# A one-token decoder step: most of W2 moves into the ring of the key and value loads, and heads 28 and 29 are loaded in smaller pieces

## The chip, the cores and the metric

The kernel runs on 1 core of a Trainium2 chip. The metric is device time in microseconds (us) of one execution; of several runs the median is taken. The profile comes from one further execution, and its times count from the first instruction of that execution (its span).

## What is computed

Two layers with the same weights, each an attention block over a cache and then an MLP, for one token of width 640 (32 heads of 128, 8192 cached positions, hidden width 1728). All is fp32.

```python
def _A_ref(x, k_cache, v_cache, wq, wo):          # x: 1 x 1 x 640
    q = (x @ wq).reshape(B, Sq, H, Dh).transpose(0, 2, 1, 3)
    scores = jnp.einsum("bhqd,bhkd->bhqk", q, k_cache) * (Dh ** -0.5)
    p = _softmax(scores, axis=-1)
    o = jnp.einsum("bhqk,bhkd->bhqd", p, v_cache)
    return o.transpose(0, 2, 1, 3).reshape(B, Sq, H * Dh) @ wo
def _B_ref(x, w1, w2):                            # hidden width 1728
    return jnp.einsum("bsf,fd->bsd", jnp.maximum(jnp.einsum("bsd,df->bsf", x, w1), 0), w2)
x = x + _A_ref(_layernorm(x), A_k_cache, A_v_cache, A_wq, A_wo)
x = x + _B_ref(_layernorm(x), B_w1, B_w2)
x = x + _A_ref(_layernorm(x), A_k_cache, A_v_cache, A_wq, A_wo)
x = x + _B_ref(_layernorm(x), B_w1, B_w2)
```

Each layer reads the whole cache once: 32 heads with 4096 KB of keys and 4096 KB of values each.

## The kernel before, in words

**Heads and units.** Layer 1 (L = 0 in the code) takes the heads 0 to 31, layer 2 (L = 1) takes them from 31 down to 0. For a head, TensorE first multiplies the query with the keys (`scores`, L336), VectorE and ScalarE make the exponentials (L347, L349), TensorE turns them (L357), and then multiplies them with the values (`values`, L390). The table `UNITS` says in which loads a head comes: `WHOLE` is one load of keys and one of values, 4096 KB each; `HALVES` is four of 2048 KB; `LAST` splits the values into 2048, 1024, 512 and 512 KB. Before the change heads 0, 1, 29, 30 and 31 come in finer loads, the others whole.

**The ring.** One SBUF tile, `ring`, takes all keys and values. It is counted in units of 4 KB (8 floats in each of 128 partitions); a head's keys are 1024 units, and the ring has 3800. `todo` lists the loads in the order of their use; `place` looks for a free stretch for the next one, and `pump` issues loads on SyncE's queue (SP) as long as one fits. A load is issued in program order, so one that doesn't fit yet holds back all behind it. `release` is called after the matmuls of a piece (one of a head's four key runs or four value blocks); it frees the piece's place and calls `pump`. In layer 1 the streamed loads use the places 0 to 3071, three loads of 1024 units.

**What is kept.** The last 3800 units of layer 1 (all of head 31, and of head 30 all but two small key loads, `DROPPED`) stay in the ring, and layer 2 begins with them without a new load. So from the end of layer 1's loads the ring is full, and the first load of layer 2 that needs a place (head 29) can be issued only when layer 2 has used the first two key pieces of head 31. The two small key loads of head 30 go beside the ring, into tiles that the MLP has finished with (`load_beside` into `mix` and `wct`, L140).

**The weights.** `wq` and `wo` are loaded by groups of four heads, W1 and W2 once, all on ScalarE's queue (ACT). W1 and W2 stay in SBUF for both layers: `w1_t`, and `w2_t` with 14 row blocks of 128 x 640 floats, 4480 KB, loaded while layer 1 is at its eighth head (L557).

**The end of a layer.** After the last head's values come its output, the last column of the projection and the hidden layer (`hidden`, L470), then 14 blocks of the product with W2 (`times_rows`, L304, into `po`) in the order 0 to 3, 12, 13, 4 to 11; between them stand two steps of the layer norm (L261, L274). One block is 4 matmuls of 160 columns (two instructions each in the trace). Then the next layer's norm and its first queries (L284) follow.

Of the kernel before, what the change touches and what calls it, by code (L numbers as in the profile page):

```python
# [10 lines left out]
F32 = mybir.dt.float32  # L11
# [4 lines left out]
P = 128  # L16
D = 640
H = 32
# [17 lines left out]
K_ALL = [(r, 0, RUN) for r in range(4)]  # L36
V_ALL = [(b, 0, 4) for b in range(NBL)]
WHOLE = [("k", K_ALL), ("v", V_ALL)]
HALVES = [("k", K_ALL[:2]), ("k", K_ALL[2:]), ("v", V_ALL[:2]), ("v", V_ALL[2:])]
LAST = [("v", V_ALL[:2]), ("v", V_ALL[2:3]), ("v", [(3, 0, 2)]), ("v", [(3, 2, 2)])]  # L40
UNITS = {h: WHOLE for h in range(H)}
UNITS[0] = HALVES[:2] + LAST
UNITS[1] = HALVES
UNITS[29] = HALVES
UNITS[30] = [
    ("k", [(0, 432, 80), (1, 0, 80)]),
    ("k", [(0, 0, 432)]),
# [1 line left out]
] + HALVES[2:]  # L49
UNITS[31] = HALVES[:2] + LAST  # L50
DROPPED = {30: 2}
RING = 3800
MIX_AT = [12, 16, 20, 24]


def wide(kind, piece):

    return 4 * piece[2] * (1 if kind == "k" else DH) // 8


def size(unit):
    return sum(wide(unit[0], piece) for piece in unit[1])
# [4 lines left out]
F_TILES = 3  # L67
F_REST = 2
FB = 4 * F_TILES + F_REST


@with_exitstack
def decode_kernel(ctx: ExitStack, tc: tile.TileContext, x, kv, wq, wo, w1, w2, out):
# [16 lines left out]
    assert sum(size(UNITS[h][i]) for h, i in kept) == RING  # L90
    todo = [(0, u) for u in order]
    todo += [(1, (h, i)) for h in range(H)[::-1] for i in range(len(UNITS[h])) if (h, i) not in kept]

    beside = todo[len(order) : len(order) + 2]
    del todo[len(order) : len(order) + 2]
    dram_at, o = {}, 0
    for h, i in order:
        dram_at[h, i] = o
        o += 8 * P * size(UNITS[h][i])
    live = {}  # L100
    at_of = {}

    def place(layer, n):


        step = 512 if n % 512 == 0 else 8
        low, high = (0, RING) if layer else ((3072, RING) if n == RING - 3072 else (0, 3072))
        at, best = low, None
        for a, m in sorted(live.values()) + [(high, 0)]:
            a = min(a, high)  # L110
            if a - at >= n and (best is None or a - at < best[1]):
                best = at, a - at
            at = max(at, -(-(a + m) // step) * step)
        return None if best is None else best[0]

    def pump():
        while todo:
            layer, u = todo[0]
            kind, pieces = unit = UNITS[u[0]][u[1]]
            n = size(unit)  # L120
            at = place(layer, n)
            if at is None:
                return
            todo.pop(0)
            o = dram_at[u]
            nc.sync.dma_start(
                ring[:, 8 * at : 8 * (at + n)],
                kv[o : o + 8 * P * n].rearrange("(p m) -> p m", p=P),
            )
            for t, piece in enumerate(pieces):  # L130
                m = wide(kind, piece)
                live[layer, u, t] = at, m
                at_of[layer, u, t] = ring, 8 * at
                at += m

    def load_beside(where, at, n):
        layer, u = beside.pop()
        kind, pieces = UNITS[u[0]][u[1]]
        assert 8 * size(UNITS[u[0]][u[1]]) == n
        nc.sync.dma_start(  # L140
            where[:, at : at + n],
            kv[dram_at[u] : dram_at[u] + P * n].rearrange("(p m) -> p m", p=P),
        )
# [49 lines left out]
    blocks = ident.rearrange("p (g r) -> p g r", g=4)[:, :, :4]  # L193
# [6 lines left out]
    all_rows = one_of_each.to_broadcast([P, P])  # L200

    w1_t = consts.tile([P, NB, DFF], F32, name="w1_t")
    w2_t = consts.tile([P, FB, D], F32, name="w2_t")
    mix = consts.tile([P, DFF], F32, name="mix")
    wct = consts.tile([P, NB, P], F32, name="wct")

# [94 lines left out]
    def times_rows(acc, wt, col, first, last):  # L301

        for g in range(4):
            nc.tensor.matmul(  # L304
                acc[32 * g : 32 * g + 32, :DR],
                col.to_broadcast([col.shape[0], 32]),
                wt[:, g * DR : (g + 1) * DR],
                start=first,
                stop=last,
                skip_group_check=True,  # L310
            )
# [167 lines left out]
    def attention_and_mlp(L, xr, s):  # L479
# [60 lines left out]
        def due(h):  # L540

            where = heads.index(h)
            k, j = divmod(where, HG)
            if j == 0:
                o_cols[k] = work.tile([P, HG], F32, name="o_cols", bufs=2)
            if where and j == 0:
                chores.append([run_out(k - 1), "pe"])
            if j == 2 and k + 1 < NG:
                slow.append([queries_of(k + 1), "pe"])
            if where == H - 2:  # L550
                chores.append([first_of_last(), "pe"])
# [18 lines left out]
        for where, h in enumerate(heads):  # L570
# [27 lines left out]
            if h == last:  # L598
                o = work.tile([P, 1], F32, name="c_ol")
# [4 lines left out]
            else:  # L604
                k, j = divmod(where, HG)
# [45 lines left out]
        nb = 4 * F_TILES  # L651
# [11 lines left out]
        po = ps_m.tile([P, 512], F32, name="px")  # L663
        blocks = list(range(4)) + [nb, nb + 1] + list(range(4, nb))
        for a, b in enumerate(blocks):
            if a == 2:
                ss = deviations(x1, s1)
            if a == 8:
                r1 = spread_of_rows(ss)
            rows = 2 * half if b == nb + 1 else P  # L670
            times_rows(
                po, w2_t[:rows, b], hT[:rows, b : b + 1], a == 0, a == len(blocks) - 1
            )

        x2 = work.tile([P, DR], F32, name="xr", bufs=2)
        s2 = work.tile([P, 1], F32, name="x_s", bufs=2)
# [7 lines left out]
    for L in range(2):  # L684
# [22 lines left out]
def _laid_out(A_x, A_k_cache, A_v_cache, A_wq, A_wo, B_w1, B_w2):  # L707
    k = np.asarray(A_k_cache)[0].reshape(H, 4, 4, RUN, DH).transpose(0, 4, 1, 2, 3)
    v = np.asarray(A_v_cache)[0].reshape(H, 4, 4, NBL, P, DH).transpose(0, 4, 1, 2, 3, 5)
    kv = np.empty(H * P * SK * 2, k.dtype)  # L710
    o = 0
    for h in range(H):
        for kind, pieces in UNITS[h]:
            n = 8 * sum(wide(kind, piece) for piece in pieces)
            block = kv[o : o + P * n].reshape(P, n)
            o += P * n
            a = 0
            for piece in pieces:
# [9 lines left out]
    w2 = np.zeros((P, FB, D), np.asarray(B_w2).dtype)  # L728
    for b, f in enumerate(_hidden_rows()):
        w2[f >= 0, b] = np.asarray(B_w2)[f[f >= 0]][:, _COLS]  # L730
    return {
        "x": np.repeat(np.asarray(A_x).reshape(D)[_COLS].reshape(4, DR), 32, axis=0),
        "kv": kv,
        "wq": np.asarray(A_wq).reshape(NB, P, NG, HG * DH).transpose(2, 1, 0, 3),
        "wo": np.asarray(A_wo)[:, _COLS].reshape(NG, HG, DH, D).transpose(0, 2, 1, 3),
        "w1": np.asarray(B_w1).reshape(NB, P, DFF).transpose(1, 0, 2),
        "w2": w2,
    }


# [22 lines left out]
```

## Time and profile before

| | |
|---|---|
| time, three runs | 1376.2, 1380.74 and 1384.16 us, median 1380.74 |
| the profiled execution | span 1375.5 us; no other time of it is given |
| TensorE (PE) busy | 996.9 us (72%), mean granted clock 0.786 |
| VectorE, ScalarE busy | 174.7 us (13%), 100.4 us (7%) |
| DMA | 571.41 MB, mean 415 GB/s over the span |
| layer 1 ends, layer 2 begins | last W2 matmul of layer 1 at 715.6 us, first keys of layer 2 at 721.1 us |

Columns of the views: a group of instructions has its line, engine, operation, output <- inputs, shape and count, then busy time and mean, then the idle time before it with what ended it. A window has its length, the busy time of each engine (with the number of instructions), the granted TensorE clock, the busy share of the 16 DMA engines and their GB/s. A DMA issue has its queue, count, size and the time from issue to landing. SPq and ACTq are the queues of SyncE and ScalarE.

### The profile page before, as it was taken

How to read it: one execution, taken by the hardware profiler on the slowest of the kernel's cores; microseconds unless marked ns; L12 is line 12 of the kernel's file. 1: busy time of each engine (PE TensorE's matmuls, PEld its weight loads, DVE VectorE, ACT ScalarE, POOL GpSimd, SP SyncE). 2: the span in 40 equal slices, each digit the busy share in tenths (PEclk: the TensorE clock that was granted, in tenths of full speed). 3: DMA queues.
4: the chain of work that ended last, by engine and by line, in shares of the span. 5: the costliest groups of instructions: out<-in, count | busy, mean ns of one | idle time of the engine just before them, and what ended most of it. 6: DMA issues, size and time to landing. Idle time of an engine off the chain costs nothing.

```text
span 1375.5 us, 15829 instructions
## 1 busy us (share of the span) xinstructions
PE 996.9 (72%) x7136; PEld 386.9 (28%) x7136; DVE 174.7 (13%) x678; ACT 100.4 (7%) x273; POOL 2.9 (0%) x10
## 2 busy tenths in 40 slices
PE   5674746677677776877788757687777677788777
PEld 2221312222222222322243222232222322232223
DVE  1010100111111111111121111011110111111111
ACT  0000000000000000000001000000000000000000
POOL 0000000000000000000000000000000000000000
PEclk9676768887887878878798887677878877687879
DMA  9999999999999999999948999999999999999994
GB/s 395 435 429 430 428 431 430 432 429 432 428 431 432 427 433 433 427 433 422 428 190 361 431 429 428 431 430 428 433 433 426 431 430 431 431 430 432 430 423 196
DMA packets 26572, 571.41 MB, mean 415 GB/s; under 512 B 2948, under 2 KB 3080, under 8 KB 4616
## 3 DMA queue, kind: packets, MB, share of 16 engines
q1 hardware_dynamic: 21896, 524.02, 88.9%
q10 hardware_dynamic: 4608, 46.37, 8.1%
q8 instruction: 56, 0.92, 0.3%
q14 instruction: 12, 0.10, 0.0%
HBM read 570.38 MB, written 0.00 MB: 415 GB/s over the span
## 4 chain that ended last, share of the span: by engine, by line
DMA 68%; PE 29%; DVE 2%; ACT 1%; issue 1%; SPq 0%; ACTq 0%; DVEq 0%
DMA ring<-in_kv 68%; PE ps L336 10%; PE outs L390 10%; PE px L457 2%; PE pt L357 2%; PE px L284 1%; PE acc L304 1%; ACT p L349 1%; DVE h_t L347 1%; PE px L304 1%; PE acc L470 1%; PE pm L377 1%; PE pm L408 0%; DVE pT L365 0%; PE px L296 0%
## 5 line engine op out<-in xcount | busy, mean ns | idle before, releaser
L336 PE MATMUL ps<-ring,spread_q 128*32 128x512 f32 (+1 forms) x2056 | 340.8, 792 | 202.9 <-DMA ring<-in_kv 202.4
L390 PE MATMUL outs<-ring,pT 128*4 128x512 f32 (+1 forms) x2080 | 329.7, 787 | 37.9 <-DMA ring<-in_kv 37.7
L336 PEld LDWEIGHTS ps<-ring,spread_q 128*32 128x32 f32 x2056 | 68.1, 136 | 351.7 <-DMA ring<-in_kv 211.3
L390 PEld LDWEIGHTS outs<-ring,pT 128*4 128x4 f32 x2080 | 57.8, 102 | 248.4 <-issue 200.0
L347 DVE TENSOR_REDUCE h_t<-ps 128x1 f32<-128x512 f32 x64 | 44.3, 692 | 498.6 <-PE ps L336 498.6
L349 ACT ACTIVATE p<-ps,h_t 128x512 f32<-128x512 f32 x64 | 44.0, 687 | 711.0 <-DVE h_t L347 700.3
L408 PE MATMUL pm<-h_t,p 128*128 128x1 f32 x512 | 68.2, 254 | 34.2 <-DVE p L403 34.2
L408 PEld LDWEIGHTS pm<-h_t,p 128*128 128x128 f32 x512 | 62.7, 190 | 96.8 <-DVE p L403 96.8
L357 PE MATMUL pt<-row_of,p 128*128 128x16 f32 x512 | 70.9, 271 | 23.0 <-ACT p L349 22.9
L357 PEld LDWEIGHTS pt<-row_of,p 128*128 128x128 f32 x512 | 64.8, 198 | 35.1 <-ACT p L349 35.1
L403 DVE COPY p<-outs 128x256 f32<-128x256 f32 x64 | 27.2, 424 | 341.9 <-PE outs L390 341.9
L370 PE MATMUL pm<-ident,h_t 128*128 128x128 f32 x128 | 31.8, 331 | 44.2 <-DVE h_t L347 44.2
L404 ACT COPY p<-outs 128x256 f32<-128x256 f32 x64 | 23.8, 372 | 480.9 <-DVE p L403 480.9
L370 PEld LDWEIGHTS pm<-ident,h_t 128*128 128x128 f32 x128 | 19.4, 190 | 103.0 <-DVE h_t L347 100.4
L457 PE MATMUL px<-w_t,wct 128*128 128x448 f32 (+1 forms) x80 | 45.8, 659 | 0.0
L377 PE MATMUL pm<-h_t 128*128 128x1 f32 x128 | 27.8, 286 | 24.5 <-DVE h_t L374 24.5
L284 PE MATMUL px<-wq_t,ln_xc 128*32 128x128 f32 x640 | 34.6, 393 | 1.4 <-DMA wq_t<-in_wq 1.4
L284 PEld LDWEIGHTS px<-wq_t,ln_xc 128*32 128x32 f32 x640 | 29.2, 165 | 20.2 <-issue 17.1
L304 PE MATMUL acc<-wo_t,o_cols 128*32 128x160 f32 x496 | 32.8, 430 | 0.0
L377 PEld LDWEIGHTS pm<-h_t 128*128 128x128 f32 x128 | 22.3, 218 | 30.8 <-DVE h_t L374 30.8
L304 PEld LDWEIGHTS acc<-wo_t,o_cols 128*32 128x32 f32 x496 | 23.0, 163 | 23.7 <-issue 18.3
L365 DVE COPY pT<-pt 128x64 f32<-128x64 f32 x64 | 14.4, 225 | 75.0 <-PE pt L357 75.0
(97 smaller groups left out, 228.7 us busy)
## 6 DMA issues: line engine op xcount, KB each, us to landing
ring<-in_kv SPq DMA_DIRECT2D x108, 4096.0 KB, 25.3
ring<-in_kv SPq DMA_DIRECT2D x27, 2048.0 KB, 27.3
wq_t<-in_wq ACTq DMA_DIRECT2D x14, 1280.0 KB, 17.1
wo_t<-in_wo ACTq DMA_DIRECT2D x14, 1280.0 KB, 17.8
w_t<-in_w ACTq DMA_DIRECT2D x1, 4480.0 KB, 24.5
w_t<-in_w ACTq DMA_DIRECT2D x1, 4320.0 KB, 24.7
ring<-in_kv SPq DMA_DIRECT2D x3, 1024.0 KB, 25.6
ring<-in_kv SPq DMA_DIRECT2D x6, 512.0 KB, 28.5
```

The source lines that it names most:

```text
L284: nc.tensor.matmul(pq[32 * j : 32 * j + 32, :DH], xc[:, c : c + 1].to_broadcast([P, 32]), wq_t[g][:, c, j * DH : (j + 1) * DH], start=(c = ...
L304: nc.tensor.matmul(acc[32 * g : 32 * g + 32, :DR], col.to_broadcast([col.shape[0], 32]), wt[:, g * DR : (g + 1) * DR], start=first, stop=last,
L336: nc.tensor.matmul(hd.ps[32 * g : 32 * g + 32, c : c + n], spread_q[:, 3 - r : 35 - r], tile_of[:, at + g * n : at + (g + 1) * n], start=f ...
L347: nc.vector.tensor_reduce(hd.nm, hd.ps, AX.X, ALU.max, negate=True)
L349: nc.scalar.activation(hd.p, hd.ps, AF.Exp, bias=hd.nm, scale=1.0, accum_out=hd.l)
L357: nc.tensor.matmul(pt[:, 16 * b : 16 * b + 16], hd.p[:, b * P : (b + 1) * P], row_of.rearrange("p g r -> p (g r)"), start=True, stop=True,)
L370: nc.tensor.matmul(pt[:, :P], hd.nm.to_broadcast([P, P]), ident, start=True, stop=True)
L377: nc.tensor.matmul(pt[:, :1], hd.l.to_broadcast([P, P]), hd.wi, start=True, stop=True)
L390: nc.tensor.matmul(hd.out[32 * g : 32 * g + 4, r : r + m].rearrange("p r d -> p (r d)"), hd.pT[:, 4 * i : 4 * i + 4], tile_of[:, v : v + m ...
L403: nc.vector.tensor_copy(oc[:, :2], hd.out[:, :2])
L408: nc.tensor.matmul(pt[:, :1], oc[:, r], hd.w[:, r : r + 1], start=(r == 0), stop=(r == 3))
L457: nc.tensor.matmul(pt[:, :n], wct[:, c], w1_t[:, c, f : f + n], start=(c == 0), stop=(c == NB - 1),)
```

## The change

Twelve of W2's fourteen blocks (3840 KB) leave the resident tile; `w2_t` keeps the last two. The ring grows by the same 960 units to 4760. The twelve blocks become four loads (4, 4, 2 and 2 blocks) that stand in `todo` behind the last values of each layer, so W2 is read from HBM twice. In layer 1 they go to the places 3800 to 4759, which nothing else uses in that layer; in layer 2 every load may take any place. When a W2 block has been multiplied, its place is released like that of a key piece, and layer 2's first loads can take it. Head 28 is now loaded in halves, and head 29 in seven loads: keys 2048, 1792 and 256 KB, values four times 1024 KB, so that its first two key loads together (960 units) are as large as W2's places.

```diff
-UNITS[29] = HALVES
+UNITS[28] = HALVES
+UNITS[29] = [
+    ("k", K_ALL[:2]),
+    ("k", [(2, 0, 512), (3, 0, 384)]),
+    ("v", V_ALL[:1]),
+    ("v", V_ALL[1:2]),
+    ("k", [(3, 384, 128)]),
+    ("v", V_ALL[2:3]),
+    ("v", V_ALL[3:]),
+]
...
-RING = 3800
+KEPT = 3800
+W2_RUNS = [range(0, 4), range(4, 8), range(8, 10), range(10, 12)]
+UNITS["w2"] = [("w", list(run)) for run in W2_RUNS]
+W2_ALL = [("w2", i) for i in range(len(W2_RUNS))]
+RING = KEPT + 4 * F_TILES * D // 8
...
+    beside = [(1, u) for u in order if u[0] == 30 and u not in kept]
+    todo = [(0, u) for u in order + W2_ALL]
+    todo += [
+        (1, (h, i))
+        for h in range(H)[::-1]
+        for i in range(len(UNITS[h]))
+        if (h, i) not in kept and h != 30
+    ]
+    todo += [(1, u) for u in W2_ALL]
...
-        low, high = (0, RING) if layer else ((3072, RING) if n == RING - 3072 else (0, 3072))
+        if layer:
+            low, high = 0, RING
+        elif u[0] == "w2":
+            low, high = KEPT, RING
+        else:
+            low, high = (3072, KEPT) if n == KEPT - 3072 else (0, 3072)
...
-    w2_t = consts.tile([P, FB, D], F32, name="w2_t")
+    w2_t = consts.tile([P, F_REST, D], F32, name="w2_t")
...
-                nc.scalar.dma_start(w2_t, w2)
+                nc.scalar.dma_start(w2_t, w2_rest)
...
-            times_rows(
-                po, w2_t[:rows, b], hT[:rows, b : b + 1], a == 0, a == len(blocks) - 1
-            )
+            if b < nb:
+                i = next(i for i, run in enumerate(W2_RUNS) if b in run)
+                where = L, ("w2", i), b - W2_RUNS[i][0]
+                tile_of, at = at_of[where]
+                wt = tile_of[:, at : at + D]
+            else:
+                wt = w2_t[:rows, b - nb]
+            times_rows(po, wt, hT[:rows, b : b + 1], a == 0, a == len(blocks) - 1)
+            if b < nb:
+                release(*where)
```

The rows below are the program's instructions on one engine, in order; a width of 8192 means 8192 floats in each of 128 partitions, or 4096 KB. On SP's queue, from the second keys of head 30 in layer 1 over the change of layers into the loads of head 29 in layer 2, there stood before:

```order
L126 DMA ring<-in_kv 128x5824
L126 DMA ring<-in_kv 128x4096 x5
L126 DMA ring<-in_kv 128x2048
L126 DMA ring<-in_kv 128x1024 x2
L140 DMA mix<-in_kv 128x1728
L140 DMA wct<-in_kv 128x640
L126 DMA ring<-in_kv 128x4096 x4
L126 DMA ring<-in_kv 128x8192 x54
```

The same place now, from the last values of head 31 to the last small load of head 29 (`in_w` is W2's twelve blocks):

```order
L153 DMA ring<-in_kv 128x2048
L153 DMA ring<-in_kv 128x1024 x2
L153 DMA ring<-in_w 128x2560 x2
L153 DMA ring<-in_w 128x1280 x2
L164 DMA mix<-in_kv 128x1728
L164 DMA wct<-in_kv 128x640
L153 DMA ring<-in_kv 128x4096
L153 DMA ring<-in_kv 128x3584
L153 DMA ring<-in_kv 128x2048 x2
L153 DMA ring<-in_kv 128x512
L153 DMA ring<-in_kv 128x2048 x2
L153 DMA ring<-in_kv 128x4096 x4
```

W2 stands between the last values and the loads into `mix` and `wct`; the four halves of head 29 have become seven loads, and the four halves behind them are head 28. At the end of the program, the same queue held before, from the last whole loads to the output:

```order
L126 DMA ring<-in_kv 128x8192 x54
L126 DMA ring<-in_kv 128x4096 x7
L126 DMA ring<-in_kv 128x2048
L126 DMA ring<-in_kv 128x1024 x2
L686 DMA out<-xr 4x160
```

and holds now:

```order
L153 DMA ring<-in_kv 128x8192 x52
L153 DMA ring<-in_kv 128x4096 x7
L153 DMA ring<-in_kv 128x2048
L153 DMA ring<-in_kv 128x1024 x2
L153 DMA ring<-in_w 128x2560 x2
L153 DMA ring<-in_w 128x1280 x2
L714 DMA out<-xr 4x160
```

So W2's second load stands behind the last values of head 0. On TensorE the product with W2 at a layer's end is the third place. Before, with the two steps of the norm between:

```order
L304 MATMUL px<-w_t,hT 32x160 x8
L261 MATMUL pm<-x_s,sel 128x1
L304 MATMUL px<-w_t,hT 32x160 x24
L274 MATMUL pm<-ln_ss,sel 128x1
L304 MATMUL px<-w_t,hT 32x160 x24
```

and now:

```order
L325 MATMUL px<-ring,hT 32x160 x8
L282 MATMUL pm<-x_s,sel 128x1
L325 MATMUL px<-ring,hT 32x160 x8
L325 MATMUL px<-w_t,hT 32x160 x8
L325 MATMUL px<-ring,hT 32x160 x8
L295 MATMUL pm<-ln_ss,sel 128x1
L325 MATMUL px<-ring,hT 32x160 x24
```

The order of the blocks is the same; twelve of them are read from the ring, the two of `w_t` stand third.

More of the change, by code (lines that the diff above doesn't have):

```diff
@@ L51 @@
 DROPPED = {30: 2}
-RING = 3800
+KEPT = 3800
 MIX_AT = [12, 16, 20, 24]
 def wide(kind, piece):
+    if kind == "w":
+        return D // 8
     return 4 * piece[2] * (1 if kind == "k" else DH) // 8
@@ L69, with decode_kernel @@
 FB = 4 * F_TILES + F_REST
+W2_RUNS = [range(0, 4), range(4, 8), range(8, 10), range(10, 12)]
+UNITS["w2"] = [("w", list(run)) for run in W2_RUNS]
+W2_ALL = [("w2", i) for i in range(len(W2_RUNS))]
+RING = KEPT + 4 * F_TILES * D // 8
 @with_exitstack
-def decode_kernel(ctx: ExitStack, tc: tile.TileContext, x, kv, wq, wo, w1, w2, out):
+def decode_kernel(ctx: ExitStack, tc: tile.TileContext, x, kv, wq, wo, w1, w2, w2_rest, out):
     nc = tc.nc
@@ L89, in decode_kernel, with place @@
     kept = [u for u in order if u[0] >= min(DROPPED) and u[1] >= DROPPED.get(u[0], 0)]
[L90 to L99, printed above, removed]
+    assert sum(size(UNITS[h][i]) for h, i in kept) == KEPT
+    beside = [(1, u) for u in order if u[0] == 30 and u not in kept]
[7 more added lines that the diff above has]
+    todo += [(1, u) for u in W2_ALL]
+    source = {}
+    for us, dram in ((order, kv), (W2_ALL, w2)):
+        o = 0
+        for u in us:
+            n = 8 * P * size(UNITS[u[0]][u[1]])
+            source[u] = dram[o : o + n].rearrange("(p m) -> p m", p=P)
+            o += n
     live = {}
     at_of = {}
-    def place(layer, n):
+    def place(layer, u, n):
         step = 512 if n % 512 == 0 else 8
-        low, high = (0, RING) if layer else ((3072, RING) if n == RING - 3072 else (0, 3072))
+        if layer:
[4 more added lines that the diff above has]
+            low, high = (3072, KEPT) if n == KEPT - 3072 else (0, 3072)
         at, best = low, None
@@ L110, in place @@
             a = min(a, high)
-            if a - at >= n and (best is None or a - at < best[1]):
-                best = at, a - at
-            at = max(at, -(-(a + m) // step) * step)
+            for base in (0, KEPT):
+                c = base + -(-max(at - base, 0) // step) * step
+                if a - c >= n and (best is None or a - at < best[1]):
+                    best = c, a - at
+            at = max(at, a + m)
         return None if best is None else best[0]
@@ L120, in pump @@
             n = size(unit)
-            at = place(layer, n)
+            at = place(layer, u, n)
             if at is None:
@@ L124, in pump @@
             todo.pop(0)
[L125 to L128, printed above, removed]
-            )
+            nc.sync.dma_start(ring[:, 8 * at : 8 * (at + n)], source[u])
             for t, piece in enumerate(pieces):
@@ L139, in load_beside @@
         assert 8 * size(UNITS[u[0]][u[1]]) == n
[L140 to L143, printed above, removed]
+        nc.sync.dma_start(where[:, at : at + n], source[u])
         for t, piece in enumerate(pieces):
@@ L670, in attention_and_mlp @@
             rows = 2 * half if b == nb + 1 else P
-            times_rows(
-                po, w2_t[:rows, b], hT[:rows, b : b + 1], a == 0, a == len(blocks) - 1
-            )
+            if b < nb:
[8 more added lines that the diff above has]
+                release(*where)
         x2 = work.tile([P, DR], F32, name="xr", bufs=2)
@@ L727, in _laid_out @@
                 a += part.shape[1]
-    w2 = np.zeros((P, FB, D), np.asarray(B_w2).dtype)
+    rows = np.zeros((P, FB, D), np.asarray(B_w2).dtype)
     for b, f in enumerate(_hidden_rows()):
-        w2[f >= 0, b] = np.asarray(B_w2)[f[f >= 0]][:, _COLS]
+        rows[f >= 0, b] = np.asarray(B_w2)[f[f >= 0]][:, _COLS]
+    w2 = np.concatenate([rows[:, run[0] : run[-1] + 1].reshape(-1) for run in W2_RUNS])
     return {
@@ L737, in _laid_out @@
         "w2": w2,
+        "w2_rest": rows[:, 4 * F_TILES :],
     }
```

## Prediction

> **What bounds the kernel now.** I read the chain of the work that ended last first, then the rate of the DMA engines over the span, then the stretches where that rate falls.
>
> ```profile
> span 1375.5 us, 15829 instructions
> DMA  9999999999999999999948999999999999999994
> GB/s 395 435 429 430 428 431 430 432 429 432 428 431 432 427 433 433 427 433 422 428 190 361 431 429 428 431 430 428 433 433 426 431 430 431 431 430 432 430 423 196
> DMA 68%; PE 29%; DVE 2%; ACT 1%; issue 1%; SPq 0%; ACTq 0%; DVEq 0%
> L336 PE MATMUL ps<-ring,spread_q 128*32 128x512 f32 (+1 forms) x2056 | 340.8, 792 | 202.9 <-DMA ring<-in_kv 202.4
> ```
>
> Two thirds of the chain are loads into the ring, and TensorE stands idle 202.4 us before the scores for them. The rate is about 430 GB/s in every slice of 34.4 us but the first, the 21st and 22nd (the change of layers) and the last (the end). So a byte that leaves the full stretches is worth its transfer time, and so is a byte that moves into one of the two gaps. The gaps, with the stretch behind the first for comparison:
>
> ```profile
> 695.00:765.00 70.00, 60.23 (x640) 29.07 (x636) 14.11 (x60) 6.15 (x18) 1.10 (x2) 0.90 0.70 280
> 765.00:840.00 75.00, 49.55 (x378) 19.89 (x374) 9.49 (x36) 5.41 (x15) 0.00 (x0) 0.81 1.00 430
> 1355.00:1375.00 20.00, 16.24 (x234) 9.57 (x226) 4.65 (x23) 1.81 (x6) 0.55 (x1) 0.99 0.12 49
> ```
>
> At the change of layers 70 us pass at 280 GB/s where 430 was possible: 70 x (1 - 280/430) = 24.4 us of lost transfer. At the end 20 x (1 - 49/430) = 17.7 us are lost. In the first gap TensorE is busy for 60 of 70 us: the MLP and the kept heads run without waiting for data, and the DMA waits for room.
>
> ```profile
> 763.52 1.90 PE ps L336 x16
> 765.44 29.05 DMA ring<-in_kv
> ```
>
> The chain leaves TensorE's own work and goes back to a load at 765.44 us. From there the DMA is the bound again, so what it has done ahead by then is worth its full time at the end.
>
> **The change, first part: W2 leaves the full stretch of layer 1.**
>
> ```profile
> w_t<-in_w ACTq DMA_DIRECT2D x1, 4480.0 KB, 24.5
> 673.82 0.33 SPq L126 DMA_DIRECT2D ring<-in_kv  x1
> ring<-in_kv SPq DMA_DIRECT2D x1, 512.0 KB, 29.7
> ```
>
> The first row is W2's load at layer 1's eighth head, in the middle of the 430 GB/s. Twelve of its 14 blocks go: 3840 KB = 3.93 MB, at 430 GB/s **9.1 us**. Everything behind it in layer 1 moves up by that. They come back behind the last values. The other two rows are that last load, issued at 673.82 and landed 29.7 us later, at 703.5. Behind it W2 takes 9.1 us, to 712.6 on the old clock; its four runs end near 706.5, 709.6, 711.1 and 712.6. When are they wanted?
>
> ```profile
> 708.81 0.48 PE L304 MATMUL px<-w_t,hT 128*32 128x160 f32 x2
> 708.90 1.27 PE L304 MATMUL px<-w_t,hT 128*32 128x160 f32 x14
> 710.61 2.88 PE L304 MATMUL px<-w_t,hT 128*32 128x160 f32 x48
> 713.74 1.84 PE L304 MATMUL px<-w_t,hT 128*32 128x160 f32 x48
> ```
>
> A block is 8 of these. The first 16 are blocks 0 and 1 (708.8); the next 48 are 2, 3, 12, 13, 4, 5, so block 4 is wanted near 712.5; the last are 6 to 11 at 0.31 us each, so 8 is wanted at 714.4 and 10 at 715.0. Each run is there 2.3 us or more before. So the wait added here costs nothing; were that cover gone, it would cost what W2 is late, 9.1 us at most.
>
> A rule of the Trainium skill speaks against this term: "DMA: Bandwidth & Descriptors", section "Where 436 GB/s comes from", has HBM bind a core near 358 GB/s. By it W2 would need 11.0 us. The slices above at 430 GB/s and more say otherwise, so the trace's rate is used; the sign would be the same.
>
> **Second part: layer 2's first loads move into the gap.** Before, the gap's queue looks thus (SyncE's issues, then the latency of a load into an idle queue, then the first whole load of head 27):
>
> ```profile
> 707.17 0.33 SPq L140 DMA_DIRECT2D mix<-in_kv  x1
> mix<-in_kv SPq DMA_DIRECT2D x1, 864.0 KB, 4.5
> 724.81 0.33 SPq L126 DMA_DIRECT2D ring<-in_kv  x1
> ring<-in_kv SPq DMA_DIRECT2D x1, 2048.0 KB, 7.5
> 748.19 0.33 SPq L126 DMA_DIRECT2D ring<-in_kv  x1
> 760.26 0.33 SPq L126 DMA_DIRECT2D ring<-in_kv  x1
> ring<-in_kv SPq DMA_DIRECT2D x1, 4096.0 KB, 23.8
> ```
>
> Head 29 starts at 724.81, when head 31's second key piece is done. 2048 KB need 4.9 us at 430 GB/s and took 7.5, so a load into an idle queue carries about 2.6 us of latency. Head 28 is one load of keys that finds its 1024 units only at 748.19, when head 30's values are done. Head 27's keys land at 760.26 + 23.8 = 784.1.
>
> Now I walk the new queue on the old clock. W2 ends at 712.6, the loads into `mix` and `wct` (1184 KB, 2.8 us) at 715.5. Head 29's first keys wait for block 6 (714.05), start at about 716.9 and end at 721.8; its second keys (1792 KB, places free at 715.6) end at 726.1, the query weights of the next group (1280 KB, ScalarE's queue) at 729.1. That is the work that W2's places make possible. Behind it each load waits for pieces that TensorE frees:
>
> ```profile
> 721.10 6.00 PE L336 MATMUL ps<-ring,spread_q 128*32 128x512 f32 x32 [0.46 <-DVE spread_q L326]
> 730.55 3.62 PE L390 MATMUL outs<-ring,pT 128*4 128x512 f32 x40
> 735.72 2.65 PE L336 MATMUL ps<-ring,spread_q 128*32 128x432 f32 x24
> 742.81 5.31 PE L390 MATMUL outs<-ring,pT 128*4 128x512 f32 x32
> 749.67 1.07 PE L336 MATMUL ps<-ring,spread_q 128*32 128x512 f32 x8
> 752.93 1.93 PE L336 MATMUL ps<-ring,spread_q 128*32 128x512 f32 x16
> ```
>
> Head 31's four key pieces (721.1 to 727.1) free head 29's next four loads (3328 KB, 7.9 us), which end at 737.0; its first value piece (731.5) frees the last one, ending at 739.4. Head 28's four halves wait for head 31's last value (734.2), head 30's kept keys (738.4), and the first and the second half of head 30's values (745.5 and 748.1). With 2.6 us of latency they are ready at 736.8, 741.0, 748.1 and 750.7, each before the load ahead has ended, and end at 744.3, 749.2, 754.1 and 759.0; the next 1280 KB of query weights make it 762.0. Head 27's keys wait for head 29's keys to be used (754.9) and land near 771.8: 12.3 us before 784.1. Bounds: the gap had 24.4 us and W2 takes 9.1, so at most 15.3 are left; the walk has 1.4 us idle before head 29 and only 1 us to spare at 748.1, and if TensorE frees each of the last four a microsecond or so late, some 4 us go, so about 8 at least. I take **12 us**, next to the walk. TensorE at a lower clock (granted 0.90 in the gap, 0.81 behind it) is in that range.
>
> TensorE must not become the bound with 12 us more data ahead. From 749.7 (head 29) to 763.5 (head 28) a head takes it 13.8 us, while 8192 KB take the DMA 19.5 us, so it gains 5.7 us per head and has caught up after some three heads of thirty. Cost 0.
>
> **Third part: W2 a second time, at the end.** Again 9.1 us, behind the last values of head 0.
>
> ```profile
> 1331.52 0.33 SPq L126 DMA_DIRECT2D ring<-in_kv  x1
> ring<-in_kv SPq DMA_DIRECT2D x1, 512.0 KB, 28.5
> 1367.10 0.72 PE L304 MATMUL px<-w_t,hT 128*32 128x160 f32 x14
> 1370.52 1.84 PE L304 MATMUL px<-w_t,hT 128*32 128x160 f32 x48
> ```
>
> The last values land at 1360.0; W2's runs end near 1363.1, 1366.1, 1367.7 and 1369.2. Blocks 0 and 1 are wanted at 1367.0, block 8 at 1371.1, block 10 at 1371.8: 2.6 us or more are left. Its places come free with heads 2 and 1, long before. Cost 0, and between 0 and 6.5 us (9.1 less the slack) if the cover fails.
>
> **Fourth part: smaller loads.** 18 more loads stand on SyncE's queue, eight of them W2's. Where a load is queued behind others, small ones are seen to cost nothing:
>
> ```profile
> ring<-in_kv SPq DMA_DIRECT2D x3, 1024.0 KB, 25.6
> ring<-in_kv SPq DMA_DIRECT2D x6, 512.0 KB, 28.5
> 25.00:35.00 10.00, 6.88 (x50) 2.33 (x50) 1.41 (x7) 0.37 (x1) 0.00 (x0) 0.83 1.03 430
> ```
>
> From 25 to 35 us head 0's values land in pieces of 1024 and 512 KB, at 430 GB/s. In an idle queue one costs the 2.6 us above. In layer 1, head 31's keys now wait for head 29's first value pieces (near 661) and not for its second keys, but they landed only at 688, so 20 us cover that. The program gives each load one of eight landing semaphores in turn, and the queue waits for the one before:
>
> ```profile
> SPq L126 <- DMA ring<-in_kv: 462.3, 115, 12.2
> ```
>
> So smaller loads reach less far ahead. The shortest reach is at head 30's second key load: the six loads ahead of it hold 4512 KB, 10.7 us, four times the latency. I take 0, with 2.6 us per load as the other end. The longer ring gives layer 2 four places of 1024 units for its stream where there were three; at 430 GB/s there is nothing for it to gain: 0.
>
> **The sum.** 1375.5 - 9.1 - 12 = 1354.4 us of span. The median of the three runs stands 5.2 us above the profiled span; with that, 1359.6, and I say 1359.5 us.
>
> **Rivals.** (1) Only W2's move pays. If TensorE frees places later than in the old trace, or the new places fragment, the queue idles as before and layer 2 gains 0 to 6 us: 1366 to 1372. For it speaks that head 29's first loads can't start before 714; against it, that 960 units of new places are there for certain. (2) The wait for W2 takes the place of the one removed: at the end, in the tail, up to 6.5 us, so 1360 to 1366. It needs W2 at below 340 GB/s. Against it stand 430 GB/s in small loads. (3) Slower: the 18 added loads each pay the 2.6 us of a lone load, 47 us in all, 1360 + 47 = 1407; it decides from 9 loads on (21.1 / 2.6). The place would be heads 28 and 29 and W2. For it speaks the 4.5 us of the lone 864 KB load, against it the row of 25 to 35 us. The Trainium skill's "DMA: Bandwidth & Descriptors", section "Measured (HBM→SBUF, 128 partitions, SWDGE, issued from GpSimd)", asks for loads of 1 MiB or more and counts 2 us for each, which is this rival; its table is of single loads, and the queue here shows the cost only where it is empty. (4) The change doesn't do what it says, W2 waiting for places of the stream: the rows of the order put it right behind the last values, and its places are unused in layer 1, so it could only come if a load ahead is held; then there is no gain, 1381.
>
> **How the numbers follow.** Forecast 70% (1353 to 1365), rival 1 15%, rival 2 7%, rival 3 4%, rival 4 4%. The range of 8 in 10 takes the forecast and the better part of rivals 1 and 2: at its low end the whole 15.3 us of the gap and a median 3 us nearer the span (1353), at its high end 2 us of gain in layer 2 (1370). Faster by over 0.5% (about what a measurement of this kernel can tell from no change) means below 1373.8: forecast, most of rival 1, rival 2, together 88%; slower 5%; within 7%.
>
> **What would show it.** In the new trace: the GB/s at 430 in the slice of the change of layers but for a few us; W2's first landing before the product's first matmul, with no DMA wait at L325 of more than a fraction; layer 2's first key load issued some 6 us before the first scores of layer 2 and not 4 us behind them; the last values of layer 1 landed 9 us earlier, those of layer 2 21 us earlier; the tail from the last values to the end still about 15.5 us. I am wrong if L325 waits for `in_w`, if SyncE's queue waits on TensorE through the gap, or if layer 1 ends where it did.

## The result, and the profile after

| | before | after |
|---|---|---|
| median, first set of runs | 1378.55 us (4 runs, 1376.2 to 1384.16) | 1362.29 us (4 runs, 1360.51 to 1364.17) |
| a second set of runs | 1379.1 us (11 runs) | 1362.19 us (6 runs) |
| ratio after to before | | 0.9879, 95% interval 0.9853 to 0.9905; second set 0.9875, 0.985 to 0.99 |
| profiled execution, span | 1375.5 us | 1362.1 us (its time: 1364.17 us) |

The kernel is faster by 16 to 17 us, 1.2%. The time lies in the range given; the gain is 4 to 5 us short of the 21.1 us that the sum had. The page of the changed kernel:

```profile
span 1362.1 us, 15890 instructions
DMA  9999999999999999999989999999999999999996
GB/s 393 431 432 430 430 430 431 428 430 431 430 430 431 428 429 434 429 428 423 428 339 426 433 430 428 431 431 429 432 430 431 428 429 432 431 434 430 428 425 266
DMA packets 29164, 575.34 MB, mean 422 GB/s; under 512 B 3236, under 2 KB 3368, under 8 KB 5800
DMA 71%; PE 26%; DVE 1%; ACT 1%; issue 0%; SPq 0%; ACTq 0%; DVEq 0%
```

4 MB more are moved (W2's second load), and yet the span is shorter: the slices 21 and 22, which had 190 and 361 GB/s, have 339 and 426, and the last has 266 for 196. The same two gaps, moved with the layer's end, by windows:

```profile
687.00:757.00 70.00, 60.66 (x628) 28.40 (x620) 13.53 (x58) 5.77 (x17) 1.10 (x2) 0.86 0.94 387
757.00:832.00 75.00, 55.13 (x426) 22.74 (x426) 10.66 (x40) 6.15 (x17) 0.00 (x0) 0.83 1.00 430
1342.00:1362.00 20.00, 15.80 (x216) 9.11 (x215) 4.04 (x21) 0.95 (x4) 0.55 (x1) 0.91 0.39 160
705.00:710.00 5.00, 4.40 (x79) 2.81 (x76) 0.55 (x3) 0.00 (x0) 0.55 (x1) 0.77 0.44 114
```

In the 70 us around the change of layers the lost transfer is 70 x (1 - 387/430) = 7.0 us, where it was 24.4. W2 filled 9.1 us of that gap, and the keys 8 to 9. The last row holds about half of what is left: 5 us at 114 GB/s, or 3.7 us of lost transfer, after W2 and before head 29's first keys.

To see where the time came from I follow a few loads. Of each pair of rows the first, of the timeline, has the time of issue, the second, of the DMA issues, the latency; the sum is the landing. In order: head 27's keys of layer 1, its last values, head 29's first keys, head 27's keys of layer 2, the last values of the kernel.

```profile
578.72 0.33 SPq L153 DMA_DIRECT2D ring<-in_kv  x1
ring<-in_kv SPq DMA_DIRECT2D x1, 4096.0 KB, 23.7
664.96 0.42 SPq L153 DMA_DIRECT2D ring<-in_kv  x1
ring<-in_kv SPq DMA_DIRECT2D x1, 512.0 KB, 30.6
707.94 0.33 SPq L153 DMA_DIRECT2D ring<-in_kv  x1
ring<-in_kv SPq DMA_DIRECT2D x1, 2048.0 KB, 8.5
748.60 0.33 SPq L153 DMA_DIRECT2D ring<-in_kv  x1
ring<-in_kv SPq DMA_DIRECT2D x1, 4096.0 KB, 18.5
1314.74 0.33 SPq L153 DMA_DIRECT2D ring<-in_kv  x1
ring<-in_kv SPq DMA_DIRECT2D x1, 512.0 KB, 29.5
```

| landed at, us | before | after | earlier by |
|---|---|---|---|
| layer 1, head 27's keys | 610.9 | 602.4 | 8.4 |
| layer 1, last values | 703.5 | 695.5 | 8.0 |
| layer 2, head 27's keys | 784.1 | 767.1 | 17.0 |
| layer 2, last values | 1360.0 | 1344.2 | 15.8 |
| end of the span | 1375.5 | 1362.1 | 13.4 |

W2 itself is nowhere waited for. Its last run in each layer, and the blocks that use it:

```profile
685.59 0.33 SPq L153 DMA_DIRECT2D ring<-in_w  x1
ring<-in_w SPq DMA_DIRECT2D x1, 640.0 KB, 19.2
707.43 1.84 PE L325 MATMUL px<-ring,hT 128*32 128x160 f32 x48
1334.32 0.33 SPq L153 DMA_DIRECT2D ring<-in_w  x1
ring<-in_w SPq DMA_DIRECT2D x1, 640.0 KB, 19.1
1357.01 1.84 PE L325 MATMUL px<-ring,hT 128*32 128x160 f32 x48
```

It lands at 704.8 and 1353.4; block 10, the fifth of these six, is multiplied at 708.7 and 1358.3.

### The profile page after: what moved, and what is told of

The parts are those of the page before. It is cut to its first block, busy times and chain, and to the rows that moved or that the text cites. A ratio compares the mean times of both kernels' runs of the same rounds, so it can differ in the third digit from the quotient of the medians.

```text
span 1362.1 us, 15890 instructions
## 1 busy us (share of the span) xinstructions
PE 995.6 (73%) x7152; PEld 387.6 (28%) x7152; DVE 174.8 (13%) x678; ACT 100.3 (7%) x273; POOL 2.9 (0%) x10
## 4 chain that ended last, share of the span: by engine, by line
DMA 71%; PE 26%; DVE 1%; ACT 1%; issue 0%; SPq 0%; ACTq 0%; DVEq 0%
DMA ring<-in_kv 71%; PE ps L357 10%; PE outs L411 7%; PE px L478 2%; PE px L305 1%; PE acc L325 1%; PE pt L378 1%; PE px L325 1%; PE acc L491 1%; PE pm L429 1%; ACT p L370 1%; DVE h_t L368 1%; PE pm L398 0%; PE px L317 0%; DVE pT L386 0%
## 5 line engine op out<-in xcount | busy, mean ns | idle before, releaser
L357 PE MATMUL ps<-ring,spread_q 128*32 128x512 f32 (+2 forms) x2072 | 331.1, 765 | 183.7 <-DMA ring<-in_kv 183.2
L411 PE MATMUL outs<-ring,pT 128*4 128x512 f32 (+1 forms) x2080 | 335.6, 799 | 44.1 <-DMA ring<-in_kv 43.7
## 6 DMA issues: line engine op xcount, KB each, us to landing
wq_t<-in_wq ACTq DMA_DIRECT2D x14, 1280.0 KB, 17.4
wo_t<-in_wo ACTq DMA_DIRECT2D x14, 1280.0 KB, 17.7
w_t<-in_w ACTq DMA_DIRECT2D x1, 4320.0 KB, 24.4
```

The source lines that it names most:

```text
L357: nc.tensor.matmul(hd.ps[32 * g : 32 * g + 32, c : c + n], spread_q[:, 3 - r : 35 - r], tile_of[:, at + g * n : at + (g + 1) * n], start=f ...
L411: nc.tensor.matmul(hd.out[32 * g : 32 * g + 4, r : r + m].rearrange("p r d -> p (r d)"), hd.pT[:, 4 * i : 4 * i + 4], tile_of[:, v : v + m ...
```

## The experiments

Two measures carry the comparisons besides the times: when layer 1's last values land, and how long from there to head 27's keys in layer 2, that is, through the whole gap. Behind it the landings keep their distance to the old ones within about 1.4 us to the end, so a microsecond in this column decides nothing. The tail is the time from the landing of the kernel's last values to the end of the span.

| kernel | median, us | layer 1's last values | from there to head 27's keys | tail after the last values |
|---|---|---|---|---|
| before / a second profile of it | 1378.6 to 1379.5 | 703.5 / 703.7 | 80.6 / 83.7 | 15.5 / 17.0 |
| finer loads alone | 1376.58 | 704.0 | 80.7 | 13.9 |
| W2 late, resident | 1368.99 | 695.0 | 81.2 | 16.6 |
| changed, old loads | 1369.30 | 694.4 | 81.8 | 14.7 |
| changed, W2 before the values | 1369.83 | 694.7 | 73.2 | 15.6 |
| changed / again | 1362.29 / 1362.19 | 695.5 / 694.8 | 71.6 / 71.7 | 17.9 / 16.6 |
| changed, small first keys | 1361.23 | 695.2 | 71.9 | 13.8 |
| changed, extra products | 1359.65 | 695.1 | 71.0 | 14.3 |
| changed, small first keys and extra products | 1359.45 | 695.5 | 71.4 | 14.2 |

**The finer loads alone.** The edit is the new `UNITS[28]` and `UNITS[29]` in the kernel before.

> The kernel before, with only heads 28 and 29 in the finer loads; W2 stays resident. Theory (W2's places carry the gain of layer 2, the finer loads only let it be used): layer 2 gains 3 to 4 us, because head 28's keys no longer wait for 1024 free units until head 30's values are done; layer 1 loses about 0.5 us (in the changed kernel its loads were 8.43 us ahead before the finer ones and 7.97 behind them). So 1374 to 1376 us against 1378.6 before. Rival (the finer loads by themselves carry layer 2's gain): 9 us, so 1369 to 1370 us.

1376.58 us, ratio 0.9977 (0.9963 to 0.9992): a gain of 1 to 5 us, 2.9 us at the medians, and not the 9 us of the rival. The theory's size fits; its time of 1374 to 1376 us is missed by 0.6 us. At head 27's keys (784.7 us, by the rows below) the gain shows only against the second profile of before (787.4), not against the first (784.1). TensorE came late: the first scores of layer 2 began 21.0 us after the last values' landing, where it was 17.6 before, with a granted clock of 0.79 in the window of that stretch. It ended head 30's values 48.0 us after that landing, as in the second profile of before (47.7) and later than in the first (44.6).

```profile
704.00:725.00 21.00, 17.96 (x250) 11.12 (x242) 4.70 (x25) 0.74 (x3) 1.10 (x2) 0.79 0.21 65
764.14 0.33 SPq L135 DMA_DIRECT2D ring<-in_kv  x1
ring<-in_kv SPq DMA_DIRECT2D x1, 4096.0 KB, 20.6
```

**W2 late, nothing else.** W2 stays resident, twelve blocks are loaded on SyncE's queue at layer 1's last head:

```diff
-                nc.scalar.dma_start(w2_t, w2)
+                nc.scalar.dma_start(w2_t[:, 4 * F_TILES :], w2[:, 4 * F_TILES :])
+            if L == 0 and where == H - 1:
+                for m, n in ((0, 4), (4, 8), (8, 10), (10, 12)):
+                    nc.sync.dma_start(w2_t[:, m:n], w2[:, m:n])
```

> The kernel before, with W2 resident in its own tile as before and loaded once, but twelve of its blocks in four loads behind layer 1's last values. It does the first part of the change alone: no second load, no new places for keys. Theory: all of the 9.0 us that W2 took in layer 1's stream, and nothing else: 1369 to 1370 us, last values of layer 1 landed about 9 us earlier, no wait of the W2 product. Rival (loads into the gap push the MLP or layer 2's first loads back): 5 us or less, so 1374 us or more, with DMA waits at the W2 product's line.

```profile
665.68 0.33 SPq L126 DMA_DIRECT2D ring<-in_kv  x1
ring<-in_kv SPq DMA_DIRECT2D x1, 512.0 KB, 29.3
754.31 0.33 SPq L126 DMA_DIRECT2D ring<-in_kv  x1
ring<-in_kv SPq DMA_DIRECT2D x1, 4096.0 KB, 21.9
```

1368.99 us, ratio 0.9921 (0.9897 to 0.9944). Layer 1's last values land at 695.0, 8.5 us earlier, and head 27's keys at 776.2, 7.9 us earlier: the gain of layer 1 goes through to the end, and the gap itself is as long as before (81.2 us). No matmul waits for W2. This is more than half of the whole change, without a second load of W2.

**W2's places, old loads.** The changed kernel with `UNITS[28]` left whole and `UNITS[29] = HALVES`.

> The changed kernel with heads 28 and 29 in the old loads (28 whole, 29 in four halves). Only one half of head 29's keys (512 units) then fits into W2's 960 places at the change of layers. Theory: layer 1's 9 us stay whole (and 0.5 us more, without its finer loads), layer 2 gains the 4.9 us of that half and little else: 1364 to 1366 us. Rival (the finer loads are not needed): as the changed kernel, 1361 to 1363 us. Rival (the finer loads carry layer 2's gain): 1369 us or more.

```profile
706.62 0.33 SPq L144 DMA_DIRECT2D ring<-in_kv  x1
ring<-in_kv SPq DMA_DIRECT2D x1, 2048.0 KB, 7.8
740.11 0.33 SPq L144 DMA_DIRECT2D ring<-in_kv  x1
ring<-in_kv SPq DMA_DIRECT2D x1, 4096.0 KB, 13.5
720.00:745.00 25.00, 20.73 (x208) 9.20 (x204) 4.79 (x18) 2.89 (x8) 0.00 (x0) 0.93 0.75 307
```

1369.30 us, ratio 0.9923 (0.9899 to 0.9947), as with W2's move alone. My expectation of 1364 to 1366 was wrong. The half of the keys that goes into W2's places lands 17.9 us earlier than before (714.4), but the 4.9 us are given back: head 28's keys come whole, find 1024 free units only at 740.1, and the queue runs at 307 GB/s from 720 to 745. TensorE was also later there than with W2 late: head 30's values ended 47.4 us after layer 1's last values, and 45.1 us there. So some 2 us of worth could hide in this profile. Together with the first experiment: finer loads alone give 1 to 5 us, W2's places alone nothing that shows beyond layer 1's part, both together 7 us more than either kernel with W2 moved. How much of these 7 us the finer loads would bring to the kernel with W2 late and resident, without new places, was not run. A load that starts earlier pays only when those behind it can follow.

**The second load ahead of the last values.** In the changed kernel's list of layer 2:

```diff
-    todo += [(1, u) for u in W2_ALL]
+    todo[-4:-4] = [(1, u) for u in W2_ALL]
```

> The changed kernel with W2's second load ahead of head 0's values and not behind them. Theory (the second load is hidden in the tail): 9 us slower than the changed kernel, 1370 to 1372 us. Rival (in the tail it cost the 2.4 us by which the tail grew in the profile, from 15.5 to 17.9 us after the last values' landing): the tail is back at about 15.5 us and the loss is 6 to 7 us, 1368 to 1369 us. If the tail stays at 17 us or more without W2 in it, W2's load was not what made it longer.

```profile
1334.33 0.33 SPq L153 DMA_DIRECT2D ring<-in_kv  x1
ring<-in_kv SPq DMA_DIRECT2D x1, 512.0 KB, 19.1
```

1369.83 us, 7.5 us slower than the changed kernel. The last values land at 1353.4 for 1344.2, 9.2 us later, W2's transfer time; the tail is 15.6 us. Ahead of the values W2 costs them its full transfer time, and behind them no matmul waits for it. The time lies between the theory's 1370 to 1372 us and the rival's 1368 to 1369, and on the tail alone the run decides nothing; the next two say more.

**The changed kernel and the kernel before, once more.**

> The changed kernel unchanged, for a second profile and more times. Theory (the tail's 17.9 us and the 18.9 us from layer 1's last values to layer 2's first scores hang on the clock that TensorE is granted there, not on the change): both differ from the first profile by a microsecond or more, with the granted clock; last values of layer 2 again 15 to 17 us earlier than before; 1361 to 1363 us. Rival (the change makes both longer): they come back within 0.5 us.

> The kernel before, for a second profile. Theory: tail after the last values' landing between 13.5 and 18 us and 17 to 21 us from layer 1's last values to layer 2's first scores, both going with the granted clock; landings elsewhere within 2 us of the first profile. Rival (before, the tail is 15.5 us and the 17.6 us are fixed): both within 0.5 us.

Head 27's keys, the last values, and head 31's values on TensorE in the second profile of before:

```profile
763.46 0.33 SPq L126 DMA_DIRECT2D ring<-in_kv  x1
ring<-in_kv SPq DMA_DIRECT2D x1, 4096.0 KB, 23.9
1335.01 0.33 SPq L126 DMA_DIRECT2D ring<-in_kv  x1
ring<-in_kv SPq DMA_DIRECT2D x1, 512.0 KB, 28.1
731.13 6.23 PE L390 MATMUL outs<-ring,pT 128*4 128x512 f32 x40
```

In the second profile of the changed kernel the last values land at 1343.1 (16.9 us earlier than in the first profile of before), with a tail of 16.6 us. The kernel before has a tail of 17.0 us this time, and the keys of its head 27 land at 787.4, 3.3 us later than in its first profile (1381.88 us, one run), where the theory allowed 2. The last row goes with that: the 40 matmuls took 3.62 us in the first profile, and all behind them came later. So before, too, tail and gap vary by 1.5 and 3 us from execution to execution. The way to the first scores came back within 0.2 us in both pairs (18.9 and 19.0 after, 17.6 and 17.4 before), which I had not expected: in the changed kernel it is 1.4 us longer in both profiles. In the other kernels with W2 in the ring it was 17.4, 17.7, 18.3, 18.9 and 20.6 us, so whether the change lengthens it stays open.

**Head 29's first keys in four loads.** In the changed kernel:

```diff
-    ("k", K_ALL[:2]),
-    ("k", [(2, 0, 512), (3, 0, 384)]),
+    ("k", K_ALL[:1]),
+    ("k", K_ALL[1:2]),
+    ("k", K_ALL[2:3]),
+    ("k", [(3, 0, 384)]),
```

> The changed kernel with head 29's first two key loads (2048 and 1792 KB) cut into four (three of 1024 KB, one of 768 KB), so that the first waits for four W2 blocks and not for nine. Theory (the 3.3 us that layer 2's part falls short of 12.3 were lost before head 29's first keys flowed): the first load is issued 3 to 4 us earlier, head 27's keys land 2 to 3 us earlier against layer 1's last values than in the changed kernel, 1359 to 1361 us. Rival (the small loads cost what they win, or the loads behind are held by TensorE's releases): within 1 us of the changed kernel.

```profile
703.47 0.33 SPq L155 DMA_DIRECT2D ring<-in_kv  x1
ring<-in_kv SPq DMA_DIRECT2D x1, 1024.0 KB, 6.4
705.00:710.00 5.00, 3.68 (x82) 3.08 (x80) 1.27 (x8) 0.00 (x0) 0.55 (x1) 1.00 0.97 378
725.00:750.00 25.00, 21.95 (x222) 9.03 (x214) 3.79 (x14) 1.82 (x5) 0.00 (x0) 0.87 0.93 362
```

The first load is issued at 703.5, and the hole of 114 GB/s is filled (378). But from 725 to 750 the queue now runs at 362 GB/s, where the changed kernel had 427, and head 27's keys land 71.9 us after layer 1's last values, as there (71.6). 1361.23 us, ratio 0.9869 (0.9846 to 0.9891): no difference that can be told. The rival holds in this run: once the hole is filled, the loads behind wait for places that TensorE frees with heads 31 and 30, and what was won at 705 is lost at 730. But TensorE was also slower here than in the changed kernel's profile. Head 31's values, in the changed kernel and in this one:

```profile
723.09 3.62 PE L411 MATMUL outs<-ring,pT 128*4 128x512 f32 x40
722.72 6.23 PE L413 MATMUL outs<-ring,pT 128*4 128x512 f32 x40
```

In the 10 us around them (from 719.5 and from 719.2) the granted clock was 1.00 and 0.66. The releases behind came some 2.6 us later, so this profile alone can't say that they bind at full clock too. The last experiment has the same loads at a higher clock.

**Extra products in the tail and in the gap.** `warm(n)` multiplies the unit matrix with itself n times into a bank that nothing reads: before the first and the third key piece of the last head (5 and 6), behind its output copy (2), and behind the projection's last column (1), in both layers. The computation is otherwise whole.

```diff
+        def warm(n):
+            pt = ps_m.tile([P, 512], F32, name="px")
+            for _ in range(n):
+                nc.tensor.matmul(pt[:, :P], ident, ident, start=True, stop=True)
...
+                if h == last and a in (0, 2):
+                    warm(5 if a == 0 else 6)
```

> The changed kernel with 14 extra 128x128 products per layer on TensorE, whose results nothing reads, in the last head and the hidden layer, where TensorE waits for data or for VectorE. Theory (the tail's length and the way from layer 1's last values to layer 2's first scores hang on granted half clock after little activity): granted clock 0.95 or more there, tail 13.5 to 14.5 us and 17.5 us to the first scores, 2 to 4 us faster than the changed kernel: 1358 to 1360 us. Rival (the half clock comes whatever TensorE does, and the extra products only lengthen the chain): clock 0.88 to 0.90 as before, the same or up to 2 us slower, 1362 to 1364 us.

> The same extra products, in the kernel with head 29's first keys in four loads. In that kernel the queue started 3.5 us earlier but then idled for TensorE's releases from 725 to 745 us. Theory (releases at TensorE's pace bound layer 2's start, and a higher clock brings them forward): 1 to 2 us faster than the extra products alone, 1357 to 1359 us. Rival (the releases hang on the heads' own length and not on the clock at the change of layers): as with the extra products alone.

The tail from the last values to the end, in the changed kernel, its second profile, the second profile of before, and with the extra products (the third column from the right is the granted clock, as a share of full speed; the first number in brackets counts the matmul instructions):

```profile
1344.00:1362.00 18.00, 14.19 (x206) 8.25 (x198) 3.29 (x17) 0.74 (x3) 0.55 (x1) 0.91 0.32 131
```
```profile
1343.00:1359.00 16.00, 12.81 (x190) 7.84 (x182) 3.30 (x17) 0.74 (x3) 0.55 (x1) 0.89 0.36 147
```
```profile
1363.00:1380.00 17.00, 13.26 (x194) 7.83 (x186) 3.30 (x17) 0.74 (x3) 0.55 (x1) 0.90 0.01 2
```
```profile
1343.00:1357.00 14.00, 10.91 (x184) 7.27 (x176) 3.30 (x17) 0.74 (x3) 0.55 (x1) 1.00 0.40 164
```

With 14 more products the tail is 14.3 us at clock 1.00, TensorE's busy time 10.9 for 14.2 us; with the small first keys it is 14.2 us, again at 1.00. 1359.65 us, ratio 0.9864 (0.9839 to 0.989), and 1359.45 us, 0.9853 (0.9833 to 0.9874): 2.5 to 2.8 us below the changed kernel at the medians, but the intervals overlap, so the gain in time is likely and not shown. The first scores came 18.3 and 17.7 us after the last values, not clearly earlier. The two tails agree with the theory that the granted clock sets the tail; but a tail of 13.8 us at 1.00 and one of 13.9 also came without the extra products, so two profiles don't prove what set the clock. Nor does the clock in the tail explain it alone, as the tail of W2 late, resident, shows:

```profile
1351.80:1368.40 16.60, 12.63 (x206) 7.50 (x194) 3.30 (x17) 0.74 (x3) 0.55 (x1) 1.00 0.00 1
```

It is 16.6 us long at 1.00, with 206 matmul instructions still to come when the last values landed. Over all eleven profiles the tails of 13.8 to 14.7 us are those with 170 to 180 of them left at that moment, and the tails of 15.5 to 17.9 us those with 190 to 206. So it also counts how far TensorE is behind when the last values come, and the extra products, most of which stand before that point, may have worked through this.

Small first keys add nothing to the time here either (1359.45 against 1359.65 us, with runs that spread over 6.5 and 9.7 us). Their profile, though, doesn't show the wait of the run before. First the 25 us from 725 with both edits, then the 70 us from layer 1's last values on, in the changed kernel, with the extra products, and with both:

```profile
725.00:750.00 25.00, 20.73 (x222) 9.94 (x214) 4.77 (x17) 2.89 (x8) 0.00 (x0) 0.93 1.01 422
695.50:765.50 70.00, 59.08 (x618) 28.06 (x610) 13.51 (x58) 6.15 (x18) 1.10 (x2) 0.88 0.94 389
695.10:765.10 70.00, 59.66 (x610) 28.53 (x602) 13.38 (x56) 6.03 (x18) 1.10 (x2) 0.85 0.97 396
695.50:765.50 70.00, 59.28 (x634) 29.06 (x630) 14.21 (x61) 6.15 (x18) 1.10 (x2) 0.90 0.98 403
```

With both, head 31's values took 3.62 us, the queue ran at 422 GB/s where it had 362, and over the 70 us it moved 403 GB/s, where the changed kernel had 389 (393 in its second profile) and the small first keys alone had 389: 0.7 to 1.0 MB more, or 1.6 to 2.3 us of transfer. Head 27's keys landed no earlier all the same (766.9 for 767.1 us), but the query weights on ScalarE's queue landed 2.9 us earlier. So the theory's 1 to 2 us can be seen in the data moved and can't be told in the time: it is neither shown nor refuted.

## Why the prediction was right, and where it was short

**The bound, and that bytes moved into the gaps pay.** Right. W2's move alone gives 8.5 us at layer 1's end and some 10 us in time.

**First term, 9.1 us for W2.** Right in mechanism, 8.0 us in this profile and 8.7 in the second. Up to head 27's keys the changed kernel was 8.4 us ahead (9.1 in the second profile), and 0.4 us went in heads 28 to 31. That loss also shows in the finer loads alone (0.4 us, with no W2 moved): it is the price of five more loads per layer that I set at 0, about 0.08 us each and far from the 2.6 us of a lone load. The rest of the first profile's shortfall was there before W2's old place: its first values landed 0.4 us later.

**Second term, 12 us for the keys in the gap.** This is the term that was mis-sized: 9.0 us measured at head 27's keys (80.6 to 71.6 us through the gap; up to 12.1 if the second profile of before is the base, so the size hangs on 3 us of spread in before itself), and 7.8 us at the last values, which landed 15.8 us earlier in all where the prediction had 21. The step that failed is the walk of the queue on the old clock. It had head 29's first keys in at 721.8 - 8.0 = 713.8; they landed at 716.4, because block 6 was multiplied 1.7 us later than in the old rows and the load took 8.5 us and not 7.5. From there to head 27's keys the queue ran without a hole, but at 424 GB/s (20,992 KB in 50.6 us) and not 430, which makes the 3.3 us whole. The small first keys then showed that this hole is not the only limit: closed in an execution where TensorE had a clock of 0.66 at head 31's values, it came back as a wait for TensorE's releases. I had named that limit (1 us to spare at 748.1) and put some 4 us on it. It is not a fixed cap: the five profiles that have both parts and W2 at the end all have 71 to 72 us in the table, but the one with small keys and a high clock had moved 1.6 to 2.3 us more data through the gap. In the six profiles with both parts the rate over the 70 us falls, but for one step of 3 GB/s, the later TensorE ends head 30's values: from 403 GB/s at 44.4 us after layer 1's last values to 381 at 49.5. So the size of the term goes with how late TensorE's releases are, and that changes from execution to execution; what the term would be at full clock throughout was not measured.

**Third term, 0 for the second load.** Right: the last values come 9.2 us later when it stands ahead of them, and behind them no matmul waits for it. The tail grew from 15.5 to 17.9 us in the profile, but without W2 in it tails of 13.9 to 17.0 us were seen, and with it 13.8 to 17.9.

**Fourth term and the rivals.** The finer loads are cheap, so the slower rival fell. Of the first rival, that only W2's move pays, half was true in a way I had not put: it is what happens without the finer loads. I had worked out their price and not their worth; the experiments show that they carry the second term together with W2's places. The 2 us for each load that rival 3 takes from the Trainium skill stand in another section of "DMA: Bandwidth & Descriptors" than the one named there, in "Anatomy of one DMA — SWDGE (gpsimd) path". The runs show no such cost for a queued load, only the 0.08 us above.

**From span to median.** I added 5.2 us, the distance of three runs' median from the profiled span. Every later profile gives both: an execution is 1.8 to 2.1 us longer than its span. The other 3 us were chance, a quick execution for the profile and a high median of three: with more runs the median of before is 1378.55 to 1379.45, and not 1380.74. Against 1379.1 the sum would have said 1358, 4 us below the result. So part of the closeness of 1359.5 to 1362.3 is luck: the base was 1.3 to 2.2 us too high, which hid as much of the second term's shortfall.

## What to carry to other kernels

A kernel at the rate of its DMA engines gains from moving a weight out of the full stretches into a stretch where the engines idle for lack of room; this alone, with W2 still read once, was more than half of the gain here. Reading it a second time cost nothing that shows where that load stood behind the last values. Room that comes free early is worth its transfer time only if the loads behind the first one are cut so that they, too, fit into what comes free next: test the two edits apart and together. And a queue that is walked on an old clock should be walked again with each release a few microseconds late: here the same 40 matmuls took 3.6 us in one execution and 6.2 us in another, and the releases behind them moved by as much.

## What the runs showed of the hardware

Two executions of one kernel agreed to 0.2 us (before) and 0.6 us (changed) over the 576 us of full DMA from head 27's keys in layer 2 to the last values. Their spans differed by 4.6 and 2.4 us: in before 3.1 us of that came in the gap and 1.5 us in the tail, in the changed kernel 1.3 us in the tail.

The 40 matmuls of head 31's values took 3.62 us where the granted clock of the 10 us around them was 1.00, and 6.23 us where it was 0.66. The tail took 13.8 to 17.9 us with the same data and work but for a few extra products; the clock alone doesn't sort it (16.6 us at 0.90 and at 1.00), the matmuls left at the landing of the last values sort short from long. On the way to layer 2's first scores clock and length don't go together in order either (17.6 us at 0.85, 18.9 at 0.90, 20.6 at 0.69).
